# Two heads to 128 partitions: another layout of tokens in a linear-attention and maxout kernel

## The chip, the cores and the metric

The kernel runs on one core of a Trainium2 chip. The metric is the device time of one execution in microseconds; lower is better. Engines are named as in the profile: PE (TensorE matmul), PEld (its weight loads), DVE (VectorE), ACT (ScalarE), POOL (GpSimd), SP (SyncE, which issues DMAs).

## The reference

Two stages. Attention with exponential features for 8 batches, 8 heads, 576 tokens of 64 numbers, and 128 features; then a feed-forward layer with a maximum of three products on 4,608 tokens of 512 numbers.

```python
def phi(x):
    proj = np.einsum('bhsd,df->bhsf', x, w_phi)
    proj = proj - np.max(np.abs(proj), axis=-1, keepdims=True)
    return np.concatenate([np.exp(proj), np.exp(-proj)], axis=-1)
q_p, k_p = (phi(q), phi(k))
kv = np.einsum('bhsf,bhsd->bhfd', k_p, v)
z = np.sum(k_p, axis=2)
num = np.einsum('bhsf,bhfd->bhsd', q_p, kv)
den = np.einsum('bhsf,bhf->bhs', q_p, z)[..., None] + 1e-06
attn = num / den
x = attn.transpose(0, 2, 1, 3).reshape(B * S, H * D)
h = np.maximum(np.maximum(x @ w1, x @ w2), x @ w3)
out = h @ w_out
```

The inputs are float32; the kernel multiplies in bfloat16 and sums in float32.

## The kernel before

**Order of the work.** Each piece of work is a node: the engines that may do it with a cost for each, the nodes and buffers it needs, and a rank. `plan` walks through time with these costs and starts, whenever an engine is free, the ready node of the lowest rank; the order that comes out is the program. The ranks are a table of numbers by unit and kind of node (RANKS), with LAGS and EVAC for the feed-forward nodes. `Queues` is the planner's picture of the two DMA queues (SP's and POOL's) with a cost per load (`pipe`) and a time per packet (`packet`). Up to 30 us, where PE has nothing else by the plan, "warm" products on a constant tile are put in (L478); later gaps of over 0.5 us get an "idler" (L977).

**Attention** works in 16 units of four heads of one batch. A unit's 2,304 tokens are 18 tiles of 128 rows. Of each head, tokens 0 to 511 are loaded as four tokens in a row of a partition (four tiles per head, 16 in all, L417 and, for q and k of units 0 to 3, which a DMA of POOL's converts on the way, L526). The last 64 tokens of each head come by loads of their own (L422) into tiles 16 and 17: each holds the last tokens of two heads, one in partitions 0 to 63, the other in 64 to 127. SP issues these loads, for two units at a time. Casts (L571) write q and k beside each other as bf16.

- T: q and k are transposed, on PE in units 0 to 3 (L584, out through DVE, L587), by a DMA later (L597).
- G: products with w_phi (L624). q lies in rows 0 to 63 and k in rows 64 to 127 of the transposed tile, so psq and psk are products of 64 rows each. The two tiles of last tokens go in one product with a block weight (L619).
- ek and r: exponents of k's products (ACT, L637) and the largest magnitudes (DVE, L643).
- E, va, vd: the factor that k's maximum makes goes onto v instead (em, L681; vab, L686 on POOL; a column of factors for z, L696). The last tokens have their own operand vtl, block-wise for two heads, filled by half-height operations (L701, L710).
- M, eq: q's products again with the maximum subtracted (psm), by an extra row of the transposed tile (L721) or, in units 0 to 3, by a product for each tile (L723, L725); exponents into Eq (L733).
- K: kv and z of two heads in one bank. Per head and sign, four products of 128 rows (L750); per two heads and sign one product of vtl with 130 columns (L753):

```python
for c in range(4):
    t = 8 * pr + 4 * ab + c
    nc.tensor.matmul(kvps()[:, ab, g, :], lhsT=Ek[g]()[:, t, :], rhs=vab()[:, g, t, :],
                     start=(g + ab + c == 0), stop=False)

nc.tensor.matmul(kvps()[:, :, g, :], lhsT=Ek[g]()[:, MT + pr, :], rhs=vt()[:, g, pr, :, :],
                 start=False, stop=(g == 1))
```

- N, x, X: the numerators and denominators (psn, L772), the division (L778, L779), and the transpose into xT (L793 on PE, L803 by DMA).

**Feed-forward** goes in nine chunks of 512 tokens: the first 512 of each batch, and last the 64 last tokens of all eight batches. The weights w2 and w3 are replaced by their differences to w1 (wd, L913), and w1 times w_out is made once (pwT L925, pm L939), so that a chunk is 48 products into ups (L833), the two relu and maximum steps (L839, L841, L843), and for each 128 tokens four products with w1 w_out (L862) and six with w_out (L867), an eviction (L875) and a store (L882). The weights are loaded by POOL's DMA queue (L484) between the loads of q and k of units 0 to 3.

Of the kernel before, what the change touches and what calls it, by code (L numbers as in the profile page):

```python
# [29 lines left out]
GROUPS = [(0, 4), (4, 4), (8, 4), (12, 4), (16, 2)]  # L30
BATCHES = [(0, 8), (8, 8), (16, 2)]
# [128 lines left out]
]  # L160
LAGS = [5.589, -10.552, 1.319, 9.794, -7.903, 7.949, 7.738, 9.54, 10.602, 10.437, 1.532, 11.4, 9.958, 7.062, 7.854, 4.266, -6.168, 11.768, 11.863, -0.019, 10.9, 6.294, -10.537, 1.844, -0.676, 9.868, -2.629]
EVAC = -24.93
# [177 lines left out]
def kernel(  # L340
# [62 lines left out]
    loaded, converted, line = {}, {}, []  # L403

    def raw_bufs(u):
        if u // 2 not in raws:
            raws[u // 2] = [buf(f"{x}_raw", 2 if x == "v" else 1, [P, 2 * UT, D], FP32) for x in "qkv"]
        return raws[u // 2]

    def load(u, n_u, what, eng, part):  # L410
        src = (q, k, v)[what]
        dst = raw_bufs(u)[what]()
        h0 = (u % 2) * HU
        heads = src[u // 2, h0:h0 + HU * n_u]
        if part == 0:
            t0 = (u % 2) * (UT + 2)
            eng.dma_start(dst[:, t0:t0 + MT, :].rearrange("p (h j) d -> p h (j d)", j=SM // P),  # L417
                          heads[:, 0:SM, :].rearrange("h (p j) d -> p h (j d)", p=P))
        else:
            tails = heads[:, SM:S, :].rearrange("(pr ab) i d -> ab i pr d", ab=2)  # L420
            for ab in range(2):
                eng.dma_start(dst[ab * D:(ab + 1) * D, MT:MT + 2 * n_u, :], tails[ab])  # L422

    def raw_part(u, what, t0, t1):
        shift = u % 2 * (2 if t0 >= MT else UT + 2)
        return raw_bufs(u)[what]()[:, shift + t0:shift + t1, :]
# [10 lines left out]
    vtl = [const.tile([P, 2, 2, 2, D + 1], BF16, name=f"vtl{i}") for i in range(NE)]  # L437
# [9 lines left out]
    def zeros():  # L447
        nc.vector.memset(w2, 0.0)
        nc.vector.memset(wphi_m, 0.0)
        nc.vector.memset(wphi_m[D:D + 1, :], -1.0)  # L450
        for i in range(NE):
            nc.vector.memset(mqp[i], 0.0)
            nc.vector.memset(vtl[i], 0.0)
            for g in range(2):
                nc.vector.memset(Eq[i][g][:, UT * P:EW], 1.0)
# [35 lines left out]
    def attention(u):  # L491
# [12 lines left out]
        mains, tails, cast, gates = [], [], {}, []  # L504
        for what in range(3):
            raw = raw_bufs(u)[what]
            if what < 2 and by_pe:
                for i, (t0, t1) in enumerate(((0, 8), (8, MT)) if u < HALVES else ((0, MT),)):
                    if u == 0 and what == 1 and K0_SP:

                        def main(t0=t0, t1=t1):
                            nc.sync.dma_start(raw_part(0, 1, t0, t1).rearrange("p (h j) d -> p h (j d)", j=SM // P),
                                              k[0, t0 // 4:t1 // 4, 0:SM, :].rearrange("h (p j) d -> p h (j d)", p=P))
# [49 lines left out]
        for i, (t0, t1) in enumerate(((MT, UT),) if by_pe else ((0, MT), (MT, UT)) if u % 2 else ((0, UT),)):  # L563
            for c in range(2):
                costs = {"POOL": 0.13 + 0.055 * (t1 - t0)}
                if by_pe:
                    costs["DVE"] = 0.35
# [441 lines left out]
```

## Time and profile before

| | |
|---|---|
| median of 3 runs | 299.7 us (299.28 to 300.21) |
| profiled execution | 299.8 us, of it 298.0 in the span |
| granted clock of PE | 1.000 |
| PE, PEld busy | 288.3 us (97%), 164.7 us (55%) |
| DVE, ACT, POOL busy | 206.6, 211.1, 133.2 us |
| DMA | 50.04 MB in 87,880 packets, 56,100 of them under 512 bytes |
| SP's queue | 62.2% of the 16 DMA engines' time |
| POOL's queue | 10.6% |

The span goes from the first to the last instruction of the program. A group line of the profile names the line of the kernel, the engine, the operation, what is written and read, the number of instructions, then busy time and mean duration, then the idle time of the engine before them and what ended it. Times of PE's products overlap: a product's record lasts until its last result is written, while the next has begun. A timeline line gives start, duration and how many instructions were merged. In a product's line the first pair of numbers (128\*128, 64\*128) is the part of the array that it uses, rows by columns.

### The profile page before, as it was taken

Reading aid. Unit: us, or ns where it says so; the run is one execution under the profiler, and the core shown is the slowest. Engines: PE = TensorE matmul, PEld = TensorE weight load, DVE = VectorE, ACT = ScalarE, POOL = GpSimd, SP = SyncE. Lnnn points to the kernel's source line nnn. Section 1 sums busy time; section 2 is a strip of 40 time slices with the busy share of each in tenths; the row PEclk is TensorE's granted clock in tenths of the full one; section 3 lists DMA queues with packets and bytes.
Section 4 is the critical chain, followed back from the end, with each engine's and each line's share of the span. In section 5 each row is a group of like instructions: output and inputs, shape, how many; then the busy total and the mean of one; then the engine's idle time right before and its main releaser. Section 6 shows DMA issues by size and latency. Waiting matters only on the chain.

```text
span 298.0 us, 7642 instructions
## 1 busy us (share of the span) xinstructions
PE 288.3 (97%) x3006; PEld 164.7 (55%) x3044; DVE 206.6 (69%) x439; ACT 211.1 (71%) x493; POOL 133.2 (45%) x150
## 2 busy tenths in 40 slices
PE   8999999999999999999999999999999999999994
PEld 3556578554655744575565546654465555444443
DVE  5994899956986988799799974778788274050230
ACT  1699889757893789997988799958969751513411
POOL 8359957490696038926486676004260600000000
PEclk9999999999999999999999999999999999999999
DMA  7999999895697999999978799964004233202005
GB/s 145 212 219 208 226 273 294 164 263 179 191 268 208 197 202 295 212 227 185 338 206 197 177 292 207 146 158 118 0 3 117 72 46 82 103 2 106 35 19 124
DMA packets 87880, 50.04 MB, mean 168 GB/s; under 512 B 56100, under 2 KB 83364, under 8 KB 87844
## 3 DMA queue, kind: packets, MB, share of 16 engines
q1 hardware_dynamic: 81684, 44.50, 62.2%
q0 software_dynamic: 6080, 4.98, 10.6%
q8 instruction: 24, 0.39, 0.6%
q14 instruction: 12, 0.10, 0.2%
q10 hardware_dynamic: 80, 0.07, 0.1%
HBM read 34.67 MB, written 9.44 MB: 148 GB/s over the span
## 4 chain that ended last, share of the span: by engine, by line
PE 79%; DMA 9%; DVE 7%; POOL 2%; issue 2%; DVEq 0%; POOLq 0%
PE ups L833 31%; PE ops L867 15%; PE ops L862 10%; DMA wout_bf<-in_moe_w_out_dram 8%; PE psn L772 5%; PE kvps L750 5%; PE psq L624 4%; PE psm L721 4%; DVE x_sb L779 2%; PE pm L939 2%; POOL qk_bf L526 1%; PE kvps L753 1%; PE psq L619 1%; DMA out_dram<-osb 1%; DVE mk L643 1%
## 5 line engine op out<-in xcount | busy, mean ns | idle before, releaser
L833 PE MATMUL ups<-xT,w_bf 128*128 128x512 bf16 x413 | 97.2, 379 | 1.4 <-DVE rden L778 0.2
L733 ACT ACTIVATE Eq<-psm 128x512 bf16<-128x512 f32 (+1 forms) x160 | 75.4, 602 | 9.3 <-PE psm L721 5.2
L686 POOL TENSOR_TENSOR vab<-v_raw,em 128x1024 bf16<-128x1024 f32 (+1 forms) x34 | 59.1, 1757 | 44.5 <-ACT em L681 31.7
L637 ACT ACTIVATE Ek<-psk 128x512 bf16<-128x512 f32 x128 | 70.3, 612 | 11.2 <-PE psk L624 11.0
L833 PEld LDWEIGHTS <-w_bf 128*128 128x128 bf16 x432 | 41.1, 98 | 46.8 <-issue 0.6
L839 DVE TENSOR_TENSOR hT<-hT,ups 128x512 bf16<-128x512 bf16 x54 | 36.8, 686 | 38.7 <-PE ups L833 36.9
L643 DVE TENSOR_REDUCE mqp<-psq 128x4 bf16<-128x512 f32 (+1 forms) x80 | 48.7, 630 | 6.4 <-PE psk L624 6.4
L867 PE MATMUL ops<-wout_bf,hT 128*128 128x512 bf16 (+1 forms) x219 | 52.4, 373 | 0.2
L875 ACT COPY osb<-ops 128x512 f32<-128x512 f32 (+1 forms) x27 | 15.6, 579 | 44.1 <-PE ops L867 43.9
L643 DVE TENSOR_REDUCE mk<-psk 128x4 f32<-128x512 f32 x64 | 43.1, 683 | 1.1 <-ACT Ek L637 1.0
L867 PEld LDWEIGHTS <-hT 128*128 128x128 bf16 x222 | 21.2, 98 | 22.7
L779 DVE TENSOR_TENSOR x_sb<-psn,rden 128x320 bf16<-128x320 f32 x64 | 31.5, 492 | 2.2
L841 ACT ACTIVATE hT<-ups 128x512 bf16<-128x512 f32 x43 | 25.8, 600 | 7.3 <-PE ups L833 6.9
L862 PE MATMUL ops<-xT 128*128 128x512 bf16 x85 | 24.0, 380 | 0.5
L772 PEld LDWEIGHTS <-Eq 128*128 128x128 bf16 x640 | 22.5, 97 | 3.1
L571 POOL CAST qk_bf<-q_raw 128x128 bf16<-128x128 f32 (+2 forms) x20 | 15.3, 781 | 19.7 <-DMA q_raw<-in_q_dram 12.3
L772 PE MATMUL psn<-kv_sb,Eq 128*128 128x65 bf16 x640 | 23.6, 193 | 0.1
L750 PE MATMUL kvps<-vab,Ek 128*128 128x65 bf16 x512 | 22.1, 194 | 0.4 <-DVE mk L643 0.4
L750 PEld LDWEIGHTS <-Ek 128*128 128x128 bf16 x512 | 20.9, 98 | 2.6 <-DVE mk L643 0.8
L624 PEld LDWEIGHTS <-qkT 64*128 64x128 bf16 x512 | 14.4, 94 | 12.4 <-issue 9.3
L701 POOL TENSOR_TENSOR vtl<-v_raw,em 64x256 bf16<-64x256 f32 x32 | 20.4, 638 | 1.2
L624 PE MATMUL psq<-w,qkT 64*128 64x128 bf16 x256 | 19.9, 217 | 0.0
(84 smaller groups left out, 323.3 us busy)
## 6 DMA issues: line engine op xcount, KB each, us to landing
v_raw<-in_v_dram SPq DMA_DIRECT2D x16, 512.0 KB, 5.7
out_dram<-osb SPq DMA_DIRECT2D x32, 256.0 KB, 2.6
q_raw<-in_q_dram SPq DMA_DIRECT2D x12, 512.0 KB, 6.8
k_raw<-in_k_dram SPq DMA_DIRECT2D x12, 512.0 KB, 5.2
w_bf<-in_moe_w_dram POOLq DMA_DIRECT2D x3, 768.0 KB, 16.5
q_raw<-in_q_dram SPq DMA_DIRECT2D x16, 64.0 KB, 12.5
k_raw<-in_k_dram SPq DMA_DIRECT2D x16, 64.0 KB, 4.6
v_raw<-in_v_dram SPq DMA_DIRECT2D x16, 64.0 KB, 5.0
```

Of the source, the lines that this page charges most:

```text
L624: nc.tensor.matmul(ps()[:, i, :], lhsT=cols[r, :], rhs=w2[r, c, :], start=True, stop=True)
L637: nc.scalar.activation(Ek[s]()[:, t0:t0 + n, :], of(1), EXP, scale=1.0 - 2.0 * s)
L643: nc.vector.tensor_reduce((mq, mk)[c]()[:, t0:t0 + n], of(c), AXX, ALU.max, apply_absolute_value=True)
L686: (nc.vector if n_.eng == "DVE" else nc.gpsimd).tensor_tensor(vab()[:, g, t0:t1, 0:D], raw_part(u, 2, t0, t1), em()[:, g, t0:t1].unsqueeze ...
L733: nc.scalar.activation(Eqb()[s][:, cols], psm()[:, 0:n * P], EXP, scale=1.0 - 2.0 * s)
L750: nc.tensor.matmul(kvps()[:, ab, g, :], lhsT=Ek[g]()[:, t, :], rhs=vab()[:, g, t, :], start=(g + ab + c == 0), stop=False)
L772: nc.tensor.matmul(psn()[:, c, :], lhsT=Eqb()[g][:, t0:t0 + P], rhs=kv()[:, pr, ab, g, :], start=(g == 0), stop=(g == 1))
L779: nc.vector.tensor_tensor(x_sb()[:, pr, :, ab, :], psn()[:, :, 0:D], rden().to_broadcast([P, 5, D]), ALU.mult)
L833: nc.tensor.matmul(ups(), lhsT=w_bf[i + 1][:, ct, j * P:(j + 1) * P], rhs=tokens_of(ct), start=(ct == 0), stop=(ct == CT - 1))
L839: nc.vector.tensor_tensor(hT()[:, j, :], hT()[:, j, :], ups(), ALU.max)
L862: nc.tensor.matmul(ops_()[:, 0:width], lhsT=tile_of(ct, tt), rhs=line_w[c_i > MOVE][:, ct, cols], start=(ct == 0), stop=False)
L867: nc.tensor.matmul(ops_()[:, 0:width], lhsT=hT()[:, j, tt * P:(tt + 1) * P], rhs=wout_bf[:, j, cols], start=False, stop=(j == JT - 1))
```

## The change

Of each head, partition i of 64 gets tokens 9i to 9i+8: nine tokens in a row, 2,304 bytes in float32. Two heads fill 128 partitions, so a unit of four heads is two pairs of nine tiles, and there are no tiles of last tokens. One load brings a tensor of a unit. The tiles that take the place of the last tokens in the grouping are the ninth tiles of both pairs (8 and 17). Each tile now holds two heads, one in the upper and one in the lower 64 rows, so kv is a sum over products of 64 rows, in turn from the upper and the lower half, each half into its own bank, and the whole unit is one node. vab covers all 18 tiles; vtl and its operations are gone. The columns that M reads are taken head by head, 64 of each tile, so that Eq has the order of before; the subtraction in units 0 to 3 is by 64 columns. The stores write the tokens back in the new order, 128 rows of 2,048 bytes each as before. The first three differences of weights are given to DVE. The planner's costs for loads and kv are new, and so are all ranks (RANKS, LAGS, EVAC), so the order of the program differs everywhere.

```diff
-GROUPS = [(0, 4), (4, 4), (8, 4), (12, 4), (16, 2)]
-BATCHES = [(0, 8), (8, 8), (16, 2)]
+NT = 9
+FULL = 1.6
+FULL_BF = 1.75
+PACKET = 105.0
+KPE = 1.2
+GROUPS = [(0, 4), (4, 4), (9, 4), (13, 4), (8, 2)]
+BATCHES = [(0, 8), (9, 8), (8, 2)]
...
-            raws[u // 2] = [buf(f"{x}_raw", 2 if x == "v" else 1, [P, 2 * UT, D], FP32) for x in "qkv"]
+            raws[u] = [buf(f"{x}_raw", 4 if x == "v" else 2, [P, UT, D], FP32) for x in "qkv"]
...
+    def rows_of(what, u, p0, p1):
         h0 = (u % 2) * HU
+        return (q, k, v)[what][u // 2, h0 + 2 * p0:h0 + 2 * p1].rearrange("(pr ab) (i c) d -> (ab i) pr (c d)", ab=2, c=NT)
...
-                mains.append(nd("Lv" if what == 2 else "L", {"SP": 0.62}, lambda what=what: load(u, n_u, what, nc.sync, 0),
-                                gates, [raw], pipe=1.7 * n_u, hold=-3.0, lat=1.7, at=what,
-                                prev=loaded.get((u - 1, what), loaded.get((u, what, "after")))))
...
-                tails.append(nd("Lw" if what == 2 else "Lt", {"SP": 1.25}, lambda what=what: load(u, 2, what, nc.sync, 1), [], [raw],
-                                pipe=0.5, hold=-2.0, lat=2.5 if by_pe else 1.7, prev=last, at=what, dmas=2, packet=36.0))
...
+                mains.append(nd("Lv" if what == 2 else "L", {"SP": 0.62}, lambda what=what, raw=raw: nc.sync.dma_start(
+                    by_pairs(raw()), rows_of(what, u, 0, 2)), gates, [raw], pipe=FULL, hold=-3.0, lat=1.7, at=what,
+                    packet=PACKET, prev=loaded.get((u - 1, what))))
...
-        vab = buf("vab", 2, [P, 2, MT, D + 1], BF16)
-        vt = fixed("vtl", vtl)
+        vab = buf("vab", 2, [P, 2, UT, D + 1], BF16)
...
-                    nc.tensor.matmul(psm()[:, 0:n * P], lhsT=wphi_m, rhs=qkT()[:, cols], start=True, stop=True)
+                rhs = tiled(qkT())[:, ts, ch]
+                    nc.tensor.matmul(psm()[:, 0:w], lhsT=wphi_m, rhs=rhs, start=True, stop=True)
...
-                for i in range(n):
-                    nc.tensor.matmul(psm()[:, i * P:(i + 1) * P], lhsT=mq()[:, t0 + i:t0 + i + 1].to_broadcast([P, P]),
-                                     rhs=minus, start=False, stop=(i == n - 1))
+                of, wide = range(UT)[ts], ch.stop - ch.start
+                for i, t in enumerate(of):
+                    nc.tensor.matmul(psm()[:, i * wide:(i + 1) * wide], lhsT=mq()[:, t:t + 1].to_broadcast([P, P]),
+                                     rhs=minus[:, ch], start=False, stop=(t == of[-1]))
...
-        for pr in range(2):
-            kvps = bank("kvps", [P, 2, 2, W])
...
-            n_k = nd("K", {"PE": 0.62}, kmm, exps[4 * pr:4 * pr + 4] + exps[8:] + n_va[pr], [vab, vt, kvps, kv] + Ek,
-                     margin=gap / 2)
+        kvps = [bank("kvps", [P, 2, 2, W]) for ab in range(2)]
+
+        def kmm():
+            for t in range(UT):
                 for g in range(2):
                     for ab in range(2):
+                        r = slice(ab * D, (ab + 1) * D)
+                        nc.tensor.matmul(kvps[ab]()[:, t // NT, g, :], lhsT=Ek[g]()[r, t, :], rhs=vab()[r, g, t, :],
+                                         start=(t + g == 0), stop=(t == UT - 1 and g == 1))
+        n_k = nd("K", {"PE": KPE}, kmm, exps + n_va, [vab, kv] + kvps + Ek, margin=gap / 2)
...
-            n_ = node("wd", 0, {"DVE": 0.6} if i else {"POOL": 1.95}, None, [w_nodes[0], w_nodes[i + 1]], [])
+            n_ = node("wd", 0, {"DVE": 0.6}, None, [w_nodes[0], w_nodes[i + 1]], [])
...
-        rows = out[b * S:b * S + SM, :].rearrange("(p j) n -> p j n", j=SM // P)
+        rows = out[b * S:(b + 1) * S, :].rearrange("(i c) n -> c i n", c=NT)
```

More of the change, by code (lines that the diff above doesn't have):

```diff
@@ L403, with tiles_of, by_pairs @@
     loaded, converted, line = {}, {}, []
+    LAST = slice(NT - 1, UT, NT)
+    def tiles_of(t0, n):
+        return LAST if n == 2 else slice(t0, t0 + n)
     def raw_bufs(u):
-        if u // 2 not in raws:
-            raws[u // 2] = [buf(f"{x}_raw", 2 if x == "v" else 1, [P, 2 * UT, D], FP32) for x in "qkv"]
[L408 to L412, printed above, removed]
-        h0 = (u % 2) * HU
[L414 to L426, printed above, removed]
+        if u not in raws:
+            raws[u] = [buf(f"{x}_raw", 4 if x == "v" else 2, [P, UT, D], FP32) for x in "qkv"]
+        return raws[u]
+    def rows_of(what, u, p0, p1):
+        h0 = (u % 2) * HU
+        return (q, k, v)[what][u // 2, h0 + 2 * p0:h0 + 2 * p1].rearrange("(pr ab) (i c) d -> (ab i) pr (c d)", ab=2, c=NT)
+    def by_pairs(t):
+        return t.rearrange("p (pr c) d -> p pr (c d)", c=NT)
     wphi_f = const.tile([P, DF], FP32, name="wphi_f")
@@ L531, in attention @@
+                    cast[what, i] = cast[what, 1] = nd("L0" if u + i == 0 and u < HALVES else "L", {"POOL": 0.85}, main, [], [qk],
+                                                       pipe=FULL_BF * (p1 - p0) / 2, lat=2.1, at=what, packet=PACKET)
                     converted.setdefault(f"{'qk'[what]}{u}", []).append(cast[what, i])
-                last = None
                 mains.append(None)
             else:
-                n_u = 1
                 if by_pe and u < len(GATES) and GATES[u]:
@@ L544, in attention @@
-                last = mains[-1]
-                loaded[u + 1, what, "after"] = last
-            if u % 2 == 0:
-                tails.append(nd("Lw" if what == 2 else "Lt", {"SP": 1.25}, lambda what=what: load(u, 2, what, nc.sync, 1), [], [raw],
-                                pipe=0.5, hold=-2.0, lat=2.5 if by_pe else 1.7, prev=last, at=what, dmas=2, packet=36.0))
-                loaded[u, what], loaded[u + 1, what, "main"] = tails[-1], mains[-1]
-                if what < 2:
-                    loaded[u + 2, what, "after"] = tails[-1]
-                loaded[u, what, "tail"] = tails[-1]
-            else:
-                tails.append(loaded[u - 1, what, "tail"])
+                    gates.append(nd("gate", {"DVE": 0.1}, lambda src=src, col=col, raw=raw: nc.vector.tensor_copy(
+                        raw()[0:1, 0, 0:1], src()[0:1, col:col + 1]), [], [src, raw]))
@@ L561, in attention, with tiled @@
                 n.prev = before
[L563 to L567, printed above, removed]
-                def do_cast(n_, c=c, t0=t0, t1=t1):
-                    dst = qk()[:, c, t0:t1, :] if by_pe else qk()[:, t0:t1, c * D:(c + 1) * D]
-                    copy_on[n_.eng](dst, raw_part(u, c, t0, t1))
-                n_ = nd("C", costs, None, [(tails if t0 else mains)[c]] + ([tails[c]] if t1 - t0 == UT else []), [(qb, kb)[c], qk])
-                n_.fn = lambda n_=n_, f=do_cast: f(n_)
-                cast[c, 2 if by_pe else i] = n_
+        for c in range(0 if by_pe else 2):
+            cast[c, 0] = nd("C", {"POOL": 0.13 + 0.055 * UT}, lambda c=c: nc.gpsimd.tensor_copy(
+                qk()[:, :, c * D:(c + 1) * D], raw_bufs(u)[c]()), [mains[c]], [(qb, kb)[c], qk])
         tr = {}
+        def tiled(t):
+            return t.rearrange("p (t c) -> p t c", c=P)
         if by_pe:
@@ L581, in tp @@
                 def tp(t0=t0, nb=nb, tps=tps):
-                    for n in range(nb):
+                    for n, t in enumerate(range(UT)[tiles_of(t0, nb)]):
                         for c in range(2):
-                            nc.tensor.transpose(tps()[c * D:(c + 1) * D, n, :], qk()[:, c, t0 + n, :], ident)
+                            nc.tensor.transpose(tps()[c * D:(c + 1) * D, n, :], qk()[:, c, t, :], ident)
                 def tc_(n_, t0=t0, nb=nb, tps=tps):
-                    copy_on[n_.eng](qkT()[:, t0 * P:(t0 + nb) * P], tps()[:, 0:nb, :].rearrange("p a c -> p (a c)"))
-                a = nd("T", {"PE": 0.08 * nb}, tp, [cast[0, i], cast[1, i], n_ident], [qk, tps])
+                    copy_on[n_.eng](tiled(qkT())[:, tiles_of(t0, nb), :], tps()[:, 0:nb, :])
+                need = [0, 1] if nb == 2 else [i]
+                a = nd("T", {"PE": 0.08 * nb}, tp, [cast[c, j] for c in range(2) for j in need if (c, j) in cast] + [n_ident],
+                       [qk, tps])
                 c_ = nd("Tc", {"DVE": 0.62 if nb == 8 else 0.22}, None, [a], [tps, qkT], locks=[tps])
@@ L615, in proj @@
                 def proj(t0=t0, n=n, psq=psq, psk=psk):
-                    for i in range(n):
-                        cols = qkT()[:, (t0 + i) * P:(t0 + i + 1) * P]
+                    for i, t in enumerate(range(UT)[tiles_of(t0, n)]):
+                        cols = qkT()[:, t * P:(t + 1) * P]
                         if n == 2:
@@ L692, in attention @@
                     costs["DVE"] = 0.08 + 0.067 * (t1 - t0)
-                n_ = va(of, "va", costs, None, [n_em, mains[2]], [vb, em, vab])
+                n_ = va("va", costs, None, [n_em, mains[2]], [vb, em, vab])
                 n_.fn = lambda n_=n_, g=g, f=v_main: f(n_, g)
-            n_ = va(of, "vd", {"ACT": 0.15, "POOL": 0.28}, None, [n_em], [em, vab])
+            n_ = va("vd", {"ACT": 0.15, "POOL": 0.28}, None, [n_em], [em, vab])
             n_.fn = lambda n_=n_, t0=t0, t1=t1: copy_on[n_.eng](vab()[:, :, t0:t1, D], em()[:, :, t0:t1])
-        def v_tail():
-            for ab in range(2):
-                r = slice(ab * D, (ab + 1) * D)
-                nc.gpsimd.tensor_tensor(
-                    vt()[r, :, :, ab, 0:D],
-                    raw_part(u, 2, MT, UT)[r].unsqueeze(1).to_broadcast([D, 2, 2, D]),
-                    em()[r, :, MT:UT].unsqueeze(3).to_broadcast([D, 2, 2, D]), ALU.mult)
@@ L705, in attention @@
-        va(range(2), "va", {"POOL": 1.25}, v_tail, [n_em, tails[2], n_const], [vb, em, vt])
-        def vd_tail(n_):
-            for ab in range(2):
-                r = slice(ab * D, (ab + 1) * D)
-                copy_on[n_.eng](vt()[r, :, :, ab, D], em()[r, :, MT:UT])
-        n_ = va(range(2), "vd", {"ACT": 0.26, "POOL": 0.52}, None, [n_em, n_const], [em, vt])
-        n_.fn = lambda n_=n_: vd_tail(n_)
-        eqs = []
-        for t0, n in GROUPS:
-            cols = slice(t0 * P, (t0 + n) * P)
+        eqs = []
@@ L722, in mm @@
                     return
-                nc.tensor.matmul(psm()[:, 0:n * P], lhsT=w2[:, 0, :], rhs=qkT()[:, cols], start=True, stop=False)
-                for i in range(n):
-                    nc.tensor.matmul(psm()[:, i * P:(i + 1) * P], lhsT=mq()[:, t0 + i:t0 + i + 1].to_broadcast([P, P]),
-                                     rhs=minus, start=False, stop=(i == n - 1))
+                nc.tensor.matmul(psm()[:, 0:w], lhsT=w2[:, 0, :], rhs=rhs, start=True, stop=False)
+                of, wide = range(UT)[ts], ch.stop - ch.start
@@ L740, in attention, with kv_out @@
         n_kvs = []
-        for pr in range(2):
-            kvps = bank("kvps", [P, 2, 2, W])
-            def kmm(pr=pr, kvps=kvps):
+        kvps = [bank("kvps", [P, 2, 2, W]) for ab in range(2)]
+        def kmm():
+            for t in range(UT):
                 for g in range(2):
                     for ab in range(2):
-                        for c in range(4):
-                            t = 8 * pr + 4 * ab + c
-                            nc.tensor.matmul(kvps()[:, ab, g, :], lhsT=Ek[g]()[:, t, :], rhs=vab()[:, g, t, :],
-                                             start=(g + ab + c == 0), stop=False)
-                    nc.tensor.matmul(kvps()[:, :, g, :], lhsT=Ek[g]()[:, MT + pr, :], rhs=vt()[:, g, pr, :, :],
-                                     start=False, stop=(g == 1))
-            def kv_out(n_, pr=pr, kvps=kvps):
-                copy_on[n_.eng](kv()[:, pr].rearrange("p a g d -> p (a g d)"), kvps().rearrange("p a g d -> p (a g d)"))
-            n_k = nd("K", {"PE": 0.62}, kmm, exps[4 * pr:4 * pr + 4] + exps[8:] + n_va[pr], [vab, vt, kvps, kv] + Ek,
-                     margin=gap / 2)
-            n_kv = nd("kv", {"DVE": 0.38, "ACT": 0.4}, None, [n_k], [kvps, kv], locks=[kvps])
+                        r = slice(ab * D, (ab + 1) * D)
+                        nc.tensor.matmul(kvps[ab]()[:, t // NT, g, :], lhsT=Ek[g]()[r, t, :], rhs=vab()[r, g, t, :],
+                                         start=(t + g == 0), stop=(t == UT - 1 and g == 1))
+        n_k = nd("K", {"PE": KPE}, kmm, exps + n_va, [vab, kv] + kvps + Ek, margin=gap / 2)
+        for ab in range(2):
+            def kv_out(n_, ab=ab):
+                copy_on[n_.eng](kv()[:, :, ab].rearrange("p r g d -> p r (g d)"), kvps[ab]().rearrange("p r g d -> p r (g d)"))
+            n_kv = nd("kv", {"DVE": 0.38, "ACT": 0.4}, None, [n_k], [kvps[ab], kv], locks=[kvps[ab]])
             n_kv.fn = lambda n_=n_kv, f=kv_out: f(n_)
@@ L781, in attention @@
                 first_eq = 4 * pr + 2 * ab
-                a = nd("N", {"PE": 0.32}, nmm, [n_kvs[pr]] + eqs[first_eq:first_eq + 2] + eqs[8:], [Eqb, kv, psn, x_sb],
+                a = nd("N", {"PE": 0.32}, nmm, [n_kvs[ab]] + eqs[first_eq:first_eq + 2] + eqs[8:], [Eqb, kv, psn, x_sb],
                        margin=gap / 3)
@@ L881, in store @@
                     for dram_ap, rows in pieces:
-                        queue.dma_start(dram_ap[:, cols], part()[rows, 0:width])
+                        queue.dma_start(dram_ap[..., cols], part()[rows, 0:width])
                 pieces = out_rows(tt)
```

79 lines of the change are left out of this document (36 added, 43 removed), and 99 rows, old and new, of the table RANKS.

## The prediction

> **What bounds the kernel now.** I read the page first, then the chain in order of time, the waits of PE, and the timeline of PE alone.
>
> ```profile
> span 298.0 us, 7642 instructions
> PE 288.3 (97%) x3006; PEld 164.7 (55%) x3044; DVE 206.6 (69%) x439; ACT 211.1 (71%) x493; POOL 133.2 (45%) x150
> L833 PE MATMUL ups<-xT,w_bf 128*128 128x512 bf16 x413 | 97.2, 379 | 1.4 <-DVE rden L778 0.2
> L701 POOL TENSOR_TENSOR vtl<-v_raw,em 64x256 bf16<-64x256 f32 x32 | 20.4, 638 | 1.2
> ```
>
> PE is the only engine near full; ACT and DVE stand at 70%, POOL below half. A busy PE holds overlapping products (379 ns long, started every 216 ns), so I go by starts. The chain says the same:
>
> ```profile
> 8.71 24.79 DMA wout_bf<-in_moe_w_out_dram
> 33.99 2.32 PE pm L939 x10
> 275.08 10.36 PE ups L833 x48
> ```
>
> Up to 33.5 us it runs through the load of w_out; from there on it is PE, product after product. How little PE waits in all:
>
> ```profile
> PE pwT L925 <- DMA w_bf<-in_moe_w_dram: 0.5, 1, 0.5
> PE pxT L793 <- DVE x_sb L779: 0.5, 2, 0.3
> PE kvps L750 <- DVE mk L643: 0.4, 1, 0.4
> PE pm L939 <- DMA wout_bf<-in_moe_w_out_dram: 0.3, 1, 0.3
> ```
>
> With the smaller rows 2.8 us; counted by late starts 3.5 to 4, nearly all before 90 us. So only PE's own work, its idle opening (64 "warm" products on no data) and these few waits make the time. Now the paces:
>
> ```profile
> 30.94 0.43 PE L750 MATMUL kvps<-vab,Ek 128*128 128x65 bf16 x8
> 31.20 0.22 PE L753 MATMUL kvps<-vtl,Ek 128*128 128x130 bf16 x1
> 31.26 0.42 PE L750 MATMUL kvps<-vab,Ek 128*128 128x65 bf16 x8
> 31.52 0.22 PE L753 MATMUL kvps<-vtl,Ek 128*128 128x130 bf16 x1
> 31.57 0.38 PE L478 MATMUL warm<-idle 128*128 128x512 bf16 x1
> ```
>
> ```profile
> 101.20 1.42 PE L772 MATMUL psn<-kv_sb,Eq 128*128 128x65 bf16 x40
> 102.46 0.44 PE L793 MATMUL pxT<-ident,x_sb 128*128 128x128 bf16 x5
> 102.83 0.23 PE L624 MATMUL psq<-w,qkT 64*128 64x128 bf16 x1
> 102.83 0.23 PE L624 MATMUL psk<-w,qkT 64*128 64x128 bf16 x1
> 102.90 0.22 PE L624 MATMUL psq<-w,qkT 64*128 64x128 bf16 x1
> ...
> 103.24 0.22 PE L624 MATMUL psk<-w,qkT 64*128 64x128 bf16 x1
> 103.38 0.45 PE L793 MATMUL pxT<-ident,x_sb 128*128 128x128 bf16 x5
> ```
>
> The first fence is half of a unit's kv: 16 products of 65 columns and 2 of 130 in 0.63 us. Those of 130 are followed after 56 ns, so one of 65 takes 32 to 33 (psn: 40 in 1.26 us, 31.5). The second has the two facts that decide the change. Products on rows 0-63 and on rows 64-127 (psq, psk) start together, and eight such pairs of 128 columns come 56 ns apart, the pace of one full-height product of 128 columns (pxT, 0.056). And a step between full height and half height costs: the last pxT starts near 102.68, psq 0.15 after it instead of 0.056, and psk is followed after 0.14 instead of 0.053. About 0.095 us each way; a 512-column product shows the same (0.312 to psq instead of 0.216).
>
> **The change, part by part.** Against the profiled execution: 299.8 us, 1.8 of them around the span of 298.0; the median of the runs is 299.7.
>
> *kv by halves.* Before, 512 products at 33 ns and 64 at 56: 16.9 + 3.6 = 20.5 us. After, 72 of 64 rows and 65 columns per unit, 1152 in all, taken in turn from both halves into two banks. As 576 pairs at the pace of the full-height row, 33 ns (pairs equal full height at 128 columns): 19.0 us, so **-1.5**. No row shows pairs of 65 columns. Below I put 30 ns (65 columns at the 0.42 ns per column of the 216 ns row, plus the 2 to 3 that 128 columns show over it): 17.3 us, 1.7 less. Above, the smallest mean spacing per product in any run of half-height products, 28 ns (16 in 0.45 us): 32.3 us, 13.3 more. I take 33, since weight loads and starts inside a pair stand 4 ns apart and fit four times into it.
>
> The Trainium skill (TensorE: Matmul & The Clock Gate, "Measured speedup vs the span model") gives a packed group the time of one product plus about 4 ns per further tile. By that a pair would take 37 ns and the sum be 2.3 us higher; the trace's pairs of 128 columns take 56, not 60, so I go by the row.
>
> *Steps between full and half height.* Before, only psq/psk and the transposes of q and k run on part of the array; the built order has 82 such steps. In the changed one kv too is half height, and nearly every kv block stands alone between full-height products: 105 steps. 23 x 0.095 = **+2.2**. This is on PE, so all of it counts. The part's bounds: 0.09 to 0.10 each, 2.1 to 2.3.
>
> *Subtraction of the maxima in units 0 to 3.* 64 products of 128 columns (56 ns, 3.6 us) become 128 of 64 columns. The nearest row is psn's, 31.5: 4.0 us, **+0.5** (+0.3 at 30). The exponent products now read q in pieces of 64 columns; the last chunk's products (48 in 10.36 us, 216 ns) read like that already: 0.
>
> *Opening.* 61 warm products for 64: 3 x 0.216 = **-0.65**.
>
> *Work off PE.* Gone are the 32 tail products on POOL (20.4 us), 32 small casts of em, the casts of last tokens (8 in units 0 to 3, 12 later), a memset pair and 24 tail loads of two DMAs each. vab grows by an eighth (1.91 to 2.15 us x 28). None of it bounds PE: **0**. What hides it is PE's backlog of chunk products, and if it had all been behind waits, the gain is at most the 2.8 us of waits. Three differences of weights go from POOL (2.13 us) to DVE (0.90): 2.7 us more there before the first ups at 51.7. DVE was busy 5.3 of 10 us from 20 to 30, which takes them; uncovered, +2.7.
>
> *Loads.* A token row was a 1,024-byte packet per four tokens; now 2,304 bytes per nine. Packets of 1,024 take 46 ns at the median, of 2,048 84, so about 94 (an estimate from these two): a unit's load of one tensor goes from 512 x 46 + 256 x 18 ns to 256 x 94 ns over 16 engines, 1.8 to 1.5 us. After 90 us nothing waits for loads: 0. In the opening SP now issues k of units 4 and 5 (1.5 us each) ahead of and behind v of unit 0, where four tail DMAs of q and k (256 packets of 18 ns over 16 engines, 0.3 each) stood. Queued behind them on SP is v, and the weights on POOL's queue share the engines: PE waited for w_1 and w_out already. From -1.5 (shorter loads) to +2 (weights later); I take 0.
>
> *kv of a unit in one block* waits for all four heads; before, the halves ran back to back anyway (30.30 to 31.57). It sits behind queued products: 0, bounds as of the opening.
>
> Sum: -1.5 + 2.2 + 0.5 - 0.65 = +0.55. 299.8 + 0.55 = **300.3**.
>
> **Rivals.**
> - *Fewer waits* (faster). For it: the waits on DVE and on loads (2.8 us by rows, up to 4), and every queue but PE's has less to do. Against: the order is written out anew, so new late ones appear. With all but 0.5 gone: 297.5.
> - *The opening slips* (slower). Weights or kv of units 0 and 1 come late behind k of units 4 and 5 and DVE's extra differences. It decides once a load lands over 1 us later than PE reaches it: w_out at 33.5 was already met with no slack. +2: 302.3.
> - *Pairs do not share the array at 65 columns* (slower; the change would not do what it says). 28 ns per product gives 300.3 + 13.3 = 313.6; two full products of 33 per pair, 319. The point from which it is slower than the measurement tells is 34 ns a pair. Against: psq/psk overlap wholly, and starts 4 ns apart.
> The Trainium skill (same page, "Wait — 56ns, not 53.3ns?") says that starts of products never come closer than about 25 ns however small they are. By that 1152 x 25 = 28.8 us and the time 310; the trace shows starts 4 ns apart inside pairs but no mean below 28, so it neither confirms nor excludes it as a mean.
>
> **How the numbers follow.** About 0.3%, or 0.9 us, is what a measurement of this kernel can tell. The sum holds within 1.2 us: 0.47, of it 0.31 within 0.9 of the median, 0.14 above, 0.02 below. Fewer waits: 0.23. The opening slips: 0.21. Pairs do not share: 0.09. So faster 0.25, same 0.31, slower 0.44. The likeliest case's own range is 299.1 to 301.5. The range for 8 in 10 takes in the lean end of fewer waits and the opening's slip with a pair of 37 ns: 297.3 to 304.0, leaving out the unshared pairs and small tails.
>
> **What would show it.** Right: kvps rows marked 64*128, two starts 4 ns apart, pairs 33 ns apart, a kv block of 1.2 us with 0.095 more on each side; PE still over 95% with the waits within 4 us; POOL near 110 us. Wrong: kvps starts a steady 25 to 28 ns apart; new rows of PE waiting for w_bf, wout_bf or vab before 60 us; or the first ups well away from 51.7 us.

## The result, and the profile after

The changed kernel takes 369.7 us (median of 4 runs, 369.11 to 370.43) beside 299.5 us (299.28 to 300.21): 1.234 times the time before, 95% interval 1.2308 to 1.2372. The forecast was 300.3 us with a range of 297.3 to 304.0; no rival came near. Times in this document are medians of all executions of a run, but ratios leave out the slow ones, those over 1.5% above the fastest of the same kernel (one each in e1, e6, e7 and e12, the last of 1,655.8 us). The page of the changed kernel, and its chain by engine:

```profile
span 368.6 us, 8790 instructions
PE 310.9 (84%) x3681; PEld 168.6 (46%) x3681; DVE 209.8 (57%) x436; ACT 208.4 (57%) x469; POOL 107.9 (29%) x91
...
PE 50%; DMA 42%; DVE 4%; ACT 2%; issue 1%; POOL 1%; SPq 0%; DVEq 0%; ACTq 0%; POOLq 0%
```

POOL is where it was forecast (107.9 us for 110), and DVE and ACT are busy within 4 us of before. What is new is that PE is 84% busy instead of 97%, and that 42% of the chain is DMA. The waits of PE in the changed kernel (engine, line, tile, what ended the wait: us in total, times, longest):

```profile
PE psm L681 <- DMA qkT<-mT: 23.8, 6, 8.5
PE ups L789 <- DMA xT<-x_sb: 10.1, 2, 5.2
PE psq L595 <- DMA qkT<-qk_bf: 6.3, 1, 6.3
PE psq L600 <- DMA qkT<-qk_bf: 4.5, 1, 4.5
PE pwT L881 <- DMA w_bf<-in_moe_w_dram: 3.3, 1, 3.3
```

Three kinds of transfers are late that do not stand among PE's waits before: the row of maxima written into qkT (L636), the DMA transposes of q and k (L573) and of the result (L759). The change edits none of their lines. The issue of the first two on SP's queue shows it too; first the changed kernel, then the kernel before (min/median/max in ns of the issuing instruction, first and last start in us):

```profile
L573 SPq DMA_TRANSPOSE qkT<-qk_bf x12: 2685/7966/11801, 54.4 to 245.5; - x12
...
L636 SPq DMA_DIRECT2D qkT<-mT x12: 787/846/7279, 83.7 to 292.9; - x12
```

```profile
L597 SPq DMA_TRANSPOSE qkT<-qk_bf x12: 2756/3586/5097, 55.5 to 191.0; - x12
...
L660 SPq DMA_DIRECT2D qkT<-mT x12: 709/803/907, 76.8 to 231.3; - x12
```

The same instructions hold SP for up to 11.8 us instead of 5.1, and one of the small rows for 7.3 instead of 0.9. What they stand behind is seen in the windows of the changed kernel (window, us; busy us of PE, PEld, DVE, ACT, POOL; granted clock; busy share of the 16 DMA engines; GB/s). Between 330 and 350 us almost nothing but stores is under way:

```profile
120.00:160.00 40.00, 28.80 (x417) 17.20 (x415) 21.30 (x52) 23.62 (x55) 14.31 (x12) 0.83 0.94 149
...
330.00:340.00 10.00, 10.00 (x48) 4.48 (x46) 4.12 (x6) 1.41 (x3) 0.00 (x0) 1.00 0.14 53
340.00:350.00 10.00, 10.00 (x48) 4.57 (x47) 0.00 (x0) 5.26 (x9) 0.00 (x0) 1.00 0.13 51
```

A share of 0.13 held for 20 us is 2 of 16 engines, and 51 GB/s is about two packets of 2,048 bytes every 84 ns. So a store now runs on two engines. By its packets (128 of 2,048 bytes, 84 to 85 ns at the median in both kernels) it takes 5.2 us; before, 16 were in flight together and a store took 0.83 us. Two at a time are in flight for 153 us of the span. Whatever shares those two engines queues behind: of the 256-byte packets after 50 us, 205 took over 3 us, 127 of them over 5, the length of a store; before, none took over 1.6.

The reason is in the access pattern. `rows[2 * tt:2 * tt + 2]` is an output side of 2 x 64 x 512 with the two c's outermost; before it was 128 x 512. The Trainium skill ("DMA: Bandwidth & Descriptors", section "🔬 Why a DMA increments its semaphore by 16 and not by 1") says that a DMA goes to the largest number of engines, up to 16, that divides the slowest dimension of both sides: here 2. The trace agrees, with its share of 0.13. A second loss follows: PE's mean granted clock is 0.93 over the run (1.00 before), and 0.83 between 120 and 160 us, where PE is idle for 11 us of 40.

### The profile page after: what moved, and what is told of

The parts are those of the page before. It is cut to its first block, busy times and chain, and to the rows that moved or that the text cites. A ratio compares the mean times of both kernels' runs of the same rounds, so it can differ in the third digit from the quotient of the medians.

```text
span 368.6 us, 8790 instructions
## 1 busy us (share of the span) xinstructions
PE 310.9 (84%) x3681; PEld 168.6 (46%) x3681; DVE 209.8 (57%) x436; ACT 208.4 (57%) x469; POOL 107.9 (29%) x91
## 4 chain that ended last, share of the span: by engine, by line
PE 50%; DMA 42%; DVE 4%; ACT 2%; issue 1%; POOL 1%; SPq 0%; DVEq 0%; ACTq 0%; POOLq 0%
PE ups L789 20%; DMA qkT<-mT 18%; DMA qkT<-qk_bf 10%; PE ops L823 8%; DMA xT<-x_sb 7%; PE ops L818 5%; DMA w_bf<-in_moe_w_dram 4%; PE psm L681 3%; PE psq L600 3%; PE kvps L710 2%; PE psn L728 2%; DMA out_dram<-osb 2%; PE warm L473 2%; PE pm L895 1%; DVE x_sb L735 1%
## 5 line engine op out<-in xcount | busy, mean ns | idle before, releaser
L789 PE MATMUL ups<-xT,w_bf 128*128 128x512 bf16 x432 | 108.8, 409 | 10.1 <-DMA xT<-x_sb 10.1
L656 POOL TENSOR_TENSOR vab<-v_raw,em 128x1152 bf16<-128x1152 f32 (+1 forms) x33 | 65.3, 2000 | 48.1 <-ACT em L652 48.1
L789 PEld LDWEIGHTS <-w_bf 128*128 128x128 bf16 x432 | 44.0, 104 | 66.2 <-issue 24.7
L619 DVE TENSOR_REDUCE mk<-psk 128x4 f32<-128x512 f32 x64 | 42.3, 682 | 6.7 <-ACT Ek L613 6.5
L681 PE MATMUL psm<-qkT,wphi_m 128*128 128x512 bf16 (+1 forms) x60 | 17.5, 421 | 23.9 <-DMA qkT<-mT 23.8
L797 ACT ACTIVATE hT<-ups 128x512 bf16<-128x512 f32 x39 | 23.3, 601 | 22.1 <-PE ups L789 21.7
L799 DVE TENSOR_SCALAR hT<-ups 128x512 bf16<-128x512 f32 x15 | 10.4, 691 | 42.6 <-PE ups L789 42.5
L544 POOL CAST qk_bf<-q_raw 128x1152 bf16<-128x1152 f32 x12 | 13.7, 1145 | 47.9 <-DMA qkT<-qk_bf 46.1
L600 PE MATMUL psq<-w,qkT 64*128 64x128 bf16 x256 | 21.0, 223 | 4.6 <-DMA qkT<-qk_bf 4.5
L728 PE MATMUL psn<-kv_sb,Eq 128*128 128x65 bf16 x640 | 23.8, 196 | 0.0
L710 PEld LDWEIGHTS <-Ek 64*128 64x128 bf16 x1152 | 19.4, 96 | 5.9 <-issue 2.1
```

Source lines behind the costliest of these rows:

```text
L600: nc.tensor.matmul(ps()[:, i, :], lhsT=cols[r, :], rhs=w2[r, c, :], start=True, stop=True)
L619: nc.vector.tensor_reduce((mq, mk)[c]()[:, tiles_of(t0, n)], of(c), AXX, ALU.max, apply_absolute_value=True)
L656: (nc.vector if n_.eng == "DVE" else nc.gpsimd).tensor_tensor(vab()[:, g, t0:t1, 0:D], vb()[:, t0:t1, :], em()[:, g, t0:t1].unsqueeze(2).t ...
L681: nc.tensor.matmul(psm()[:, 0:w], lhsT=wphi_m, rhs=rhs, start=True, stop=True)
L728: nc.tensor.matmul(psn()[:, c, :], lhsT=Eqb()[g][:, t0:t0 + P], rhs=kv()[:, pr, ab, g, :], start=(g == 0), stop=(g == 1))
L789: nc.tensor.matmul(ups(), lhsT=w_bf[i + 1][:, ct, j * P:(j + 1) * P], rhs=tokens_of(ct), start=(ct == 0), stop=(ct == CT - 1))
```

## The experiments

Ratios are to the kernel before on the same chip, with 95% intervals.

| run | what differs | us | ratio |
|---|---|---|---|
| e1_store_split | changed kernel, store as 2 DMAs of 64 rows | 307.3 | 1.022 (1.017 to 1.026) |
| e2_before_two | kernel before, store 2 x 64 x 512 | 369.4 | 1.231 (1.228 to 1.234) |
| e10_before_four | kernel before, store 4 x 32 x 512 | 319.8 | 1.066 (1.063 to 1.069) |
| e3_store_act | changed kernel, stores on ACT's queue | 365.1 | 1.219 (1.214 to 1.224) |
| e4_token_first | changed kernel, another token order | 351.7 | 1.173 (1.168 to 1.177) |
| e8_old_ranks | e1, ranks of before | 355.4 | 1.186 (1.180 to 1.191) |
| e5_wd_pool | e1, three differences on POOL | 307.3 | 1.023 (1.020 to 1.027) |
| e6_k_late | e1, k of units 4, 5 behind v of unit 1 | 306.9 | 1.020 (1.015 to 1.025) |
| e7_all_three | e5 + e6 + fourth difference later | 304.2 | 1.011 (1.008 to 1.014) |
| e11_k_later_alone | e1, k of units 4, 5 behind v of unit 2 | 303.5 | 1.011 (1.008 to 1.015) |
| e9_k_later | e7 with the k loads of e11 | 301.25 | 1.003 (1.0015 to 1.0046) |
| e12_next_to_g | e9 with 95 steps between full and half height for 105 | 300.9 | 1.003 (1.000 to 1.005) |

**e1: the store alone.**

```diff
-lambda tt, rows=rows: [(rows[2 * tt:2 * tt + 2], slice(0, P))], 1)
+lambda tt, rows=rows: [(rows[2 * tt + i], slice(i * D, (i + 1) * D)) for i in range(2)], 1)
```

> The changed kernel with each chunk store written as two DMAs of 64 rows instead of one whose output side is 2 x 64 x 512; the order of all other instructions is that of the changed kernel. Theory A (a store whose slowest dimension is 2 runs on 2 of the 16 DMA engines, holds them 5.2 us instead of 0.8, and what stands behind it on those engines, the rows of the maximum and the transposes, comes late): the stores spread again over 15 to 16 engines, PE's waits for DMA fall from 48 us to a few us, time 297 to 303 us. Rival B (the new order puts loads ahead of the transposes and rows of the maximum on SP's queue): stays above 355. Rival C (packets of 2,304 bytes hold up the transposes): stays above 355.

307.3 us: 62.4 of the 70 us are gone with two 64 x 512 DMAs in place of one of 2 x 64 x 512, the same rows and the same packets. The waits of PE in this run:

```profile
PE pwT L881 <- DMA w_bf<-in_moe_w_dram: 2.3, 1, 2.3
PE psm L683 <- DVE x_sb L735: 1.4, 1, 1.4
PE pxT L749 <- DVE x_sb L735: 1.3, 3, 0.6
PE kvps L710 <- issue: 1.1, 1, 1.1
```

Not one wait on mT, on the transposes or on xT is left. The span falls by 61.6 us, and the pages of the two runs split this: PE is idle for 57.7 us in the changed kernel and for 15.3 here, which is 42 us of waits. The other 19 us fit the clock: its mean of 0.930 over 368.6 us and of 0.987 over 307.0 us are at most 25.8 and 4.0 us of full speed lost (an estimate from these means).

7.5 us remain by the medians, 6.4 by the ratio. Part of that is the clock as well: in e1's profile it is halved twice before the end, for 3.4 us each time, first 1.2 us after PE's wait for w_1 has ended, then amid the waits on x_sb (columns as in the windows above).

```profile
22.70:26.10 3.40, 3.40 (x23) 1.73 (x17) 2.31 (x4) 2.14 (x5) 0.00 (x0) 0.50 1.15 255
53.40:56.80 3.40, 2.86 (x24) 1.66 (x25) 3.29 (x8) 2.02 (x5) 0.82 (x1) 0.50 0.52 44
```

Three executions of e1 at a mean clock of 1.000 take 304.9 to 305.8 us, two at 0.983 and 0.987 take 309.3 and 308.9: the median of 307.3 lies between two groups.

**e2 and e10: the same fault in the kernel before.** Only the way the output side is written changes (a=4, p=32 in e10); the rows of a batch land in another order.

```diff
-rows = out[b * S:b * S + SM, :].rearrange("(p j) n -> p j n", j=SM // P)
+rows = out[b * S:b * S + SM, :].rearrange("(a j p) n -> j a p n", a=2, p=D)
...
-lambda tt, rows=rows: [(rows[:, tt, :], slice(0, P))], 1)
+lambda tt, rows=rows: [(rows[tt], slice(0, P))], 1)
```

> The kernel before, its order untouched, with the chunk stores' output side written as 2 x 64 x 512 (the rows of a chunk land in another order, same rows and bytes). Theory A: the stores run two packets at a time, 5 us each, and the kernel slows by about what the change cost; its own order has the same 12 transposes and 12 rows of the maximum between the stores, so 350 to 385 us. Rivals B and C (the new order, the larger packets): no store of theirs is involved, so within 1% of 299.7 us.

> The kernel before with the output side of the store written 4 x 32 x 512 (with 2 x 64 x 512 it took 369.4 us); the rows of a batch land in another order. Theory 'the slowest dimension of the output side sets how many of the 16 engines carry a store': 128 packets of 84 ns on four engines, 2.7 us each, so about 77 us of the span with a store in flight in place of 152; the waits of TensorE behind the stores fall by more than half: 305 to 330 us. Rival 'any written-out third dimension costs the full price (the order of the rows)': about 369 us.

369.4 us with two, 319.8 us with four. The waits of PE on the row of maxima, first with two, then with four:

```profile
PE psm L721 <- DMA qkT<-mT: 53.4, 9, 11.7
```

```profile
PE psm L721 <- DMA qkT<-mT: 13.0, 6, 3.5
```

With four, the busy share while only stores run is 0.25, four of 16 engines:

```profile
290.00:300.00 10.00, 10.00 (x48) 4.56 (x47) 0.00 (x0) 5.10 (x9) 0.00 (x0) 1.00 0.25 68
```

The new layout, the new ranks and the size of the packets are not needed for the harm: the store alone brings it, and its price falls from 69.6 to 19.8 us when the slowest dimension doubles. Four stores in a row take 12.4 and 14.3 us there, so one takes 3.1 to 3.6 us and not the 2.7 expected, since the packets are slower than 84 ns (119 in the mean between 290 and 300 us). That a store of this length mostly hides under PE's backlog, where one of 5.2 us does not, is the likely reading; it was not tried by itself. A third dimension as such does not bring the price: the store of e4 below, 16 x 8 x 512, has one too and takes 1.3 us.

**e3: the engines or SP's queue?**

```diff
-lambda f=store, pieces=pieces: f(nc.sync, pieces)
+lambda f=store, pieces=pieces: f(nc.scalar, pieces)
```

> The changed kernel with its two-engine stores issued from ACT instead of SP, at the same places of the order. It tells whether the harm is the queue (what stands behind a store on SP's rings waits for it) or the two engines themselves. If the queue: rows of the maximum and transposes no longer stand behind stores, PE's waits fall below 15 us, time 300 to 320 us (ACT gives 0.4 to 0.6 us per store). If the engines themselves are full: 32 stores x 5.2 us still hold two of 16 engines for 166 us, a transposing load needs its turn on them, time stays above 340 us. Rivals B and C: above 355.

365.1 us. The waits of PE:

```profile
PE ups L789 <- DMA xT<-x_sb: 11.0, 3, 6.0
PE psq L600 <- DMA qkT<-qk_bf: 10.1, 1, 10.1
PE psm L681 <- DMA qkT<-mT: 6.4, 1, 6.4
PE psq L595 <- DMA qkT<-qk_bf: 5.3, 2, 2.8
```

The wait on mT falls from 23.8 to 6.4 us, those on the transposes grow. The issue on SP's queue in this run, for the lines shown above:

```profile
L573 SPq DMA_TRANSPOSE qkT<-qk_bf x12: 2727/8647/15508, 53.3 to 245.6; - x12
L636 SPq DMA_DIRECT2D qkT<-mT x12: 738/767/907, 78.1 to 287.9; - x12
```

The small rows go out as fast as before, and of the 256-byte packets only 20 take over 3 us, none over 3.3. So the packets of 5 us go with the queue that the stores stand in. But the transposes hold SP as long as in the changed kernel, with no store on their queue, and the time is almost the same. The two full engines are the cause; the queue only chooses which transfer meets them.

**e4: tokens ordered so that one DMA spreads.** Output columns of M in the order i, c; the store is 16 x 8 x 512.

```diff
+                if wide == D:
+                    rhs = rhs.rearrange("p t c -> p c t")
...
-lambda tt, rows=rows: [(rows[2 * tt:2 * tt + 2], slice(0, P))], 1)
+lambda tt, rows=rows: [(rows[16 * tt:16 * tt + 16, 0:NT - 1], slice(0, P))], 1)
```

> The changed kernel with the order of tokens inside a chunk turned (partition first, then the eight tokens in it), by reading q's columns for the subtraction with a step of one tile, so that one store is 16 x 8 x 512 and can use 16 engines without a second DMA. Theory A: stores as fast as before the change, time 297 to 303 us as with two DMAs, unless PE's products that read with a step (64 of 512 columns in units 0 to 3 and as many after, 216 ns each now) run slower: at half pace 64 x 0.216 = 14 us more, about 313. Rivals B and C: above 355.

351.7 us, with PE 97% busy: the stores are as short as in e1, but M pays. The lines of psm in this run (min/median/max ns):

```profile
L690 PE MATMUL psm<-minus,mqp x136: 219/247/247, 15.8 to 78.0; 128*128 128x64 bf16 x128, 128*128 128x128 bf16 x8
L684 PE MATMUL psm<-qkT,wphi_m x60: 272/1040/1040, 98.1 to 291.9; 128*128 128x512 bf16 x48, 128*128 128x256 bf16 x12
```

From start to start, a 512-column product whose moving operand is read in steps of 256 bytes takes 861 ns instead of 216. 64 of them are 41.3 us; 128 products of M whose output is stepped take 56 ns instead of 29, 3.5 us. Without both the run would stand at 307 us, where e1 does.

**The other 7.5 us.** A late start is one that comes later than the pace of the product before it. Those that e1 has beyond the kernel before lie mostly in the first 60 us. Two events stand out: the load of w_1, the first weights of the feed-forward layer, lands at 21.4 us (18.2 before), and a difference of weights holds DVE while PE waits for unit 1's divisions. Five runs on top of e1 move these alone; PE's order stays, instruction by instruction.

> The changed kernel with its store in two DMAs (307.3 us), and the first three weight differences back on POOL, where they stood before; every other instruction keeps its place. Theory 'the opening lost its slack' (late first weight, DVE's extra work, and their echo in TensorE's clock): only the DVE part of it goes, TensorE's idle time between 20 and 40 us falls by at most 1 us, time 305.5 to 307.5. Rival 'DVE's three extra differences are the 7.5 us' (the prediction's uncovered price was 2.7 us): 304.5 or less. Rival 'the loss lies in the new layout, all along the kernel': no change, 307.3.

> The changed kernel with its store in two DMAs (307.3 us), and k of units 4 and 5 loaded on SP at 15 us instead of ahead of v of units 0 and 1 (the cast of unit 4's k on POOL and the load of unit 6's k move behind them); TensorE's order stays. Theory 'the opening lost its slack': the first load of w_1 lands about 3 us earlier (21.4 to 18.5 us), the wait of 2.4 us at 19 us and part of the low clock after it go, time 303 to 305.5. Rival 'the loss lies in the new layout, all along the kernel': w_1 lands earlier and the end does not move, 306.5 to 308.

> The edits of the two before it together, and the fourth weight difference on DVE moved from 44 us of the plan, ahead of unit 1's divisions, to 50.6, next to the fifth. Theory 'the opening lost its slack': TensorE's idle time in the first 60 us falls from about 12.7 us to near the 5.2 us of the kernel before, time 300 to 303. Rival 'the loss lies in the new layout, all along the kernel': 305 or more.

> As the run with all three edits of the opening (304.2 us), but k of units 4 and 5 now stands behind v of unit 2 on SP, which went out at 20 us (in the runs before, SP still issued both by 9 us, and w_1 landed at 21.4 to 21.8 us as it did without the edit); their casts on POOL, and the loads of k of units 6 and 8, move back with them. Theory 'w_1 is late because 1.15 MB of k share the engines with it': w_1 lands at 17 to 18.5 us, TensorE's wait of 3.5 us for it falls under 1 us, TensorE's idle time between 0 and 40 us falls from 8.7 to about 5 us, time 300 to 302. Rival 'w_1 is late by POOL's own queue, what SP loads does not matter': it lands at 21 us again, 304.

> Only the moves of the k loads and casts of the run that took 301.25 us; the first three weight differences are back on DVE and the fourth stands ahead of unit 1's divisions, as in the changed kernel with the store in two DMAs (307.3 us). The run with the three differences alone on POOL took 307.3 us, so they seem to cost nothing by themselves. Theory 'the late w_1 is most of it, the fourth difference the rest': w_1 lands at 18.4 us, the waits behind the fourth difference (1.55 and 0.74 us at 50 to 53 us) stay: 303 to 304.5 us. Rival 'w_1 alone': 301 to 302.

e5 changes nothing beyond the intervals (about 1.4 us each way): the three extra differences on DVE are hidden, as the sum had it. e6 did not do what it was meant to: SP reached the moved loads at 7 and 9 us, w_1 landed at 21.4 us again, and the time stayed. In e9 and e11 the loads stand behind v of unit 2, go out after 20 us, and w_1 lands at 18.4 and 18.8 us. By the medians that is 3.9 us of the 7.5 (e11: 3.7 above its kernel before), by the ratios 3.1 of 6.4. With the fourth difference moved too (and the first three on POOL, which e5 prices at 0), 1.2 us are left (e9). DVE in e1 and, below, POOL in e1 (start, us) show what this difference met:

```profile
48.79 2.37 DVE L869 TENSOR_TENSOR w_bf<-w_bf 128x1024 bf16<-128x1024 bf16 x1
56.98 0.68 DVE L869 TENSOR_TENSOR w_bf<-w_bf 128x1024 bf16<-128x1024 bf16 x1
```

```profile
48.49 4.65 POOL L656 TENSOR_TENSOR vab<-v_raw,em 128x1152 bf16<-128x1152 f32 x2
```

The difference takes 0.68 us alone and 2.37 us beside POOL's products of v: it ends 0.54 us after the first of them ends (51.16 and 50.62 us). The divisions queued behind it on DVE (x_sb) then let PE wait 1.4 us, and start 0.74 us late once more. e7 (three edits, but w_1 late) lies between. The halved clock goes with the waits: e5, e6 and e7, where w_1 is late, have a stretch of 3.4 us at 0.50 from 22.2, 21.0 and 22.0 us, e11 one from 49.6 us, after a wait of 1.8 us for x_sb. In e9 the clock is 1.00 throughout, and the longest wait of PE, 1.0 us, stands at the start of the program.

**e8: the old ranks.**

> The changed kernel with its store in two DMAs (307.3 us), and the ranks, lags and evacuation value of the kernel before: the whole order is drawn anew, in all stages. Theory 'the opening lost its slack by its order, the layout itself is worth about -1 us': an order made with the old ranks avoids the early k loads but fits the new nodes by chance, 301 to 309. Rival 'the layout costs the 7.5 us whatever the order': 306 to 309 with idle time spread over all stages. This run can only speak against the rival, by a time under 304.

355.4 us, far outside the 301 to 309 expected; it settles nothing on the layout. The old ranks are numbers for other nodes, and the order that comes out leaves PE gaps in the plan that are filled with a hundred products on nothing (two in e1):

```profile
L934 PE MATMUL idler<-idle 128*128 128x512 bf16 x100 | 28.2, 380 | 6.3 <-ACT Eq L695 1.7
```

**e12: the price of a step between full and half height (mode step).** Four kv blocks or projections and a transpose moved by a step so that half-height work meets half-height work.

> The run that took 301.25 us, with the kv blocks of units 4, 11 and 15 moved by one step of TensorE's order next to a projection of half height, the projection of unit 10 moved next to the kv block of unit 9, and one transpose of unit 4 moved out from between a kv block and a projection: 95 mode steps in place of 105, the products are the same. Theory 'a mode step costs 0.095 us of TensorE's time': 10 x 0.095 = 0.95 us less, 299.9 to 300.7. Rival 'the time at a mode step is hidden anyway, or the moved work comes late': 301.25 or more.

300.9 us beside 301.25: the intervals (1.0002 to 1.0054 and 1.0015 to 1.0046) cover each other, so the 0.95 us are neither confirmed nor excluded as time. Neither run beats the kernel before.

## Why the prediction was wrong

**The step that failed** is the one that is not in it: the stores have no term. The text before the prediction says that they write "128 rows of 2,048 bytes each as before"; that holds for the packets and says nothing of how many engines share them. Every load and the opening were costed as packets over 16 engines; the store was not looked at, because its bytes and packets stay. It is worth +69.6 us in the kernel before (e2) and 62.4 us in the changed one (e1): on two engines a store lasts 5.2 us instead of 0.83.

**"After 90 us nothing waits for loads: 0"** rested on short transfers. It did not ask what a longer transfer in the same queues would do to the rows and transposes that PE does need there; 44.7 us of waits on these are the four first lines of the waits after.

**The opening** was the right place with the wrong size. The prediction named k of units 4 and 5 ahead of w_1 with -1.5 to +2 and took 0; e11 puts it at 3 to 4 us. It named DVE's three extra differences with 0, uncovered +2.7; e5 says 0. What it did not see is the fourth, which it counted as unchanged: the order drawn anew set it beside POOL's product and ahead of the divisions. The rival "the opening slips" (+2) so had its mechanism right and about a third of its price; the halved clock after a wait was in neither. Two signs that the prediction named for being wrong did show, and both point at the opening alone: a row of 3.3 us waits for w_bf, and the first ups starts at 55.5 us instead of 51.7. Nothing among these signs points at the stores; that PE would stay over 95% busy with its waits within 4 us, named as a sign of being right, did not come true (84%, 52 us).

**PE's own terms held, within their bounds.** A kv block in e9, where no clock is lost, and the products before it (start, us, engine, line, how many):

```profile
140.87 1.46 PE L823 MATMUL ops<-wout_bf,hT 128*128 128x512 bf16 x6
142.26 1.27 PE L710 MATMUL kvps<-vab,Ek 64*128 64x65 bf16 x72
```

Starts inside a pair are 3 to 4 ns apart; 72 products start within 1.08 us, so a pair takes 30.4 ns, near the lower bound of 30 and below the 33 taken; the term is about -3 in place of -1.5. The rival "pairs do not share" falls. The Trainium skill's floor of about 25 ns from start to start ("TensorE: Matmul & The Clock Gate", section "Wait — 56ns, not 53.3ns?"), on which the prediction put 310 us, does not hold here, not even as a mean: 1.08 us over 71 steps are 15 ns. The steps to and from half height cost 0.095 us in the starts (512-column product to kvps 0.311 instead of 0.216), as forecast. The products of 64 columns in M start 29 ns apart, for 31.5 taken: +0.1 in place of +0.5.

With store and opening mended (e9) the time is 301.25, 0.3% above before, within the range of the forecast, which was 300.3. That is in part luck, since two misses cancel: by starts (products missing in the record of before counted at 216 ns) e9 has about 3 us less of PE's work than before, where the sum had 1.65 less, and 2.2 more of steps, as forecast; so about 2 more are left for late starts, which the sum put at nothing. The largest single one, 0.74 us, lies inside a kv block at 117 us and is put down to "issue". Its cause was not tried.

## What to carry to other kernels

When a layout changes, write out both sides of every DMA, the stores included, and look at the slowest dimension: the same bytes in the same packets took six times as long because it fell from 128 to 2. A transfer that holds two of 16 engines delays every other transfer that uses them, so its price shows up in the waits of innocent lines; a steady DMA share of 1/8 in the windows is the sign. If one write cannot have a slowest dimension that reaches all 16 engines (16, 64 and 128 did here), split it into DMAs that do, and do not buy it with a stepped moving operand on PE.

## What the runs showed of the hardware

- The number of engines of a store of 256 KB follows the slowest dimension: 5.2 us at 2, 3.1 to 3.6 at 4, 1.3 at 16 (e4), 0.83 at 128, and a DMA share of 0.13 at 2 and 0.25 at 4. Two DMAs of 64 rows take 1.4 us together (e1).
- The granted clock falls to 0.50 in stretches of 3.4 us, or of two or three times that, late in a wait of PE or soon after it: at 22.7 and 53.4 us in e1, at 49.6 in e11, in ten places of the changed kernel before its end, and nowhere in e9. It is not certain: e5 has the wait of 1.4 us for x_sb at 52 us and no such stretch after it.
- A 512-column product with a moving operand in steps of 256 bytes takes 861 ns instead of 216, four times as long.
- A bf16 difference of 128 x 1024 on DVE takes 0.68 us alone. Started while a POOL product or cast of SBUF tiles runs, it ends 0.54 us after that one's end: 2.37 us in e1 and e5, 2.41 in e11, 1.32 in e9. The POOL product begun meanwhile took 2.57 us (median 2.12). The Trainium skill ("SBUF — State Buffer", section "🔬 SBUF: two separate sides") says that the two share a pair of ports that one of them holds for a whole instruction while the other is blocked; the trace agrees.
- Pairs of half-height products of 65 columns start 30.4 ns apart, one product each 15 ns; a step between full and half height costs 0.095 us.
